# Row softmax without TensorE transposes for five batches, attention pieces placed behind the second product, and pair sums queued later

## The chip, the cores and the metric

The kernel runs on one core of a Trainium2 chip. The time is the device time of one execution in microseconds (us), the median of several runs. Engines: TensorE (PE; its weight loads are listed apart as PEld), VectorE (DVE), ScalarE (ACT), GpSimd (POOL) and SyncE (SP, which issues the DMAs here).

## The reference

```python
# attention between x [B=8, H=8, S=512, D=64] and state [B, H, Ns=32, D]
scores = scale * x @ state.T                    # [.., 512, 32], softmax over the 32 states
xread  = softmax(scores) @ state
scores2 = scale * state @ x.T                   # [.., 32, 512], softmax over the 512 tokens
sread  = softmax(scores2) @ x
y = concat([xread, sread], axis=2)              # then [B*544, 512] = [4352, 512]
h = relu(y @ w_in);  y = (h * h) @ w_out        # w_in 512x2048, w_out 2048x512
out = ((y @ w1) * (y @ w2)) @ w3 @ w_out2       # w1, w2 512x1024, w3 1024x1024, w_out2 1024x512
```

The weights come as 64-bit floats, x and state as 32-bit ones; the output is float32, 4352 x 512.

## The kernel before

All matrices are used as a high and a low part (`split`, L79: a ScalarE copy makes the high part, a VectorE subtraction the low part), and a product is three TensorE passes over these parts, 128x128 weights against 512 columns. The framework makes the order of each engine's instructions: it takes them by their place in the program text, but an instruction whose inputs are not ready in its model may be passed by a later one; on the chip each engine then runs its own list strictly in that order. `tc.issue_after(ins)` queues the instructions of a block that run on the engine of `ins` behind `ins`; instructions of the block on other engines are left alone.

**First stage.** The work goes in turns i = 0 to 143 over (c, f): c is a group of 512 token rows (one batch of `xread`, the ninth group is all of `sread`) and f one of 16 slices of 128 hidden columns. A turn does `h_tile(c, f)` (first product, six matmuls for c < 8, tile `ph`), then the jobs of `side[i]`, then `y_tile` of the turn two earlier (second product, twelve matmuls, tile `y`). From turn 32 on, c = i // 16. The side jobs are

- `conv` (L496): conversion of a 128x512 block of 64-bit weights by five VectorE and one or two ScalarE instructions, in every second turn from turn 24 on;
- `make_sw` (L349): product of the states with a block of `w_in`, sixteen matmuls of 64x32 weights into two PSUM banks, in turns f = 1, 5, 9, 13;
- the attention of batch b, spread by `att_slots(b)` (L336) over the sixteen turns of group c = b - 1, for b = 2 to 7. In slots 0 to 3 `xpose` (four TensorE transposes, `ps_x`), in 4 `scores`, in 5 and 7 `soft2`, in 7 and 11 `soft1a` (four transposes, `ps_n`, then two VectorE instructions), in 8 and 12 `soft1b`, in 10 and 13 `a_T` (four transposes, `ps_a`, then a `split`), in 6 and 10 `a2_T` (four transposes), in 8 and 11 `sread` (sixteen small matmuls), in 9 and 12 `sread_T` (one transpose). These steps stand in front of the other side jobs of their turn.

All of these pieces take their PSUM from one pair of banks, `bank_m` (L70, two buffers). A piece can start only when ScalarE or VectorE has emptied the bank that it gets; `make_sw` wants both.

The scores tile `S` holds, per half r, 4 heads x 32 states on the partitions and 512 tokens on the free axis. `soft1a` turns it so that tokens lie on the partitions and 32 states lie side by side on the free axis, and reduces over these 32.

**Last stage.** Groups go in pairs (2,3), (4,5), (6,7), (0,1), once for each half s of the hidden columns, in the second half in the opposite order. For a pair, `load_pair` (L667) reads eight blocks of y into two `wi1` buffers. Groups 0 and 1 lie in three parts each, so their pair also reads 16 further blocks through two `pt` buffers, which GpSimd adds (L676). `make_pair` (L680) makes seven sums and differences with eight VectorE subtractions and fourteen `split`s, 22 VectorE instructions in all. Four `quad`s (L714, m = 0 to 3, 42 matmuls each) multiply, and `out_tile` (L793, eight per pair, 12 matmuls each, two PSUM banks) makes the outputs. `load_pair` of the next pair stands behind quad m = 1, its `make_pair` behind the first of the eight output tiles; `make_w` stands there in place of `make_pair` between the halves.

Of the kernel before, what the change touches and what calls it, by code (L numbers as in the profile page):

```python
# [8 lines left out]
F32 = mybir.dt.float32  # L9
# [11 lines left out]
def kernel(  # L21
# [17 lines left out]
    nc = tc.nc  # L39
    B, H, S, D = x.shape  # L40
    NS = state.shape[2]
# [4 lines left out]
    P = 128  # L46
    G = 2
    HG = H // G
    J = S // P
    NF = DF // P  # L50
# [3 lines left out]
    NT9 = B * NS  # L54
    scale = 1.0 / float(D) ** 0.5
    HI, LO = 0, 1

    def f32(ap):
        return ap.bitcast(F32)
# [6 lines left out]
    ident = const.tile([P, P], F32, name="ident")  # L66
# [3 lines left out]
    def bank_m(name):  # L70
        return psum.tile([P, 512], F32, tag="m", bufs=2, name=name)
# [91 lines left out]
    def make_win0(half, kk):  # L163
        if win_t[0] is None:
            win_t[0] = wpool.tile([P, ND, 512], F32, tag="wi0", bufs=2, name="win0")
        convert64(("win0", half, kk), win_t[0][:, 2 * kk:2 * kk + 2, half * 256:(half + 1) * 256])
# [55 lines left out]
    def att_steps(b):  # L222
# [3 lines left out]
        v = {}  # L226
# [39 lines left out]
            v["a2", r] = e  # L266

        def soft1a(r):
            ps = bank_m("ps_n")
            for j in range(J):  # L270
                nc.tensor.transpose(ps[:, j * P:(j + 1) * P], v["S", r][:, j * P:(j + 1) * P], ident)
            pv = ps.rearrange("p (k n) -> p k n", n=NS)
            mx = att.tile([P, J * HG, 1], F32, tag="mx", bufs=2, name="mx")
            nc.vector.tensor_reduce(out=mx, in_=pv, axis=AX.X, op=ALU.max)
            e = att.tile([P, J * HG, NS], F32, tag="e1", bufs=1, name="e1")
            nc.vector.tensor_tensor(out=e, in0=pv, in1=mx.to_broadcast([P, J * HG, NS]), op=ALU.subtract)
            v["e1", r] = e

# [7 lines left out]
            nc.vector.tensor_tensor(out=e, in0=e, in1=sm.to_broadcast([P, J * HG, NS]), op=ALU.mult)  # L286

        def a_T(r):
            ps = bank_m("ps_a")
            e = v["e1", r].rearrange("p k n -> p (k n)")  # L290
            for j in range(J):
                nc.tensor.transpose(ps[:, j * P:(j + 1) * P], e[:, j * P:(j + 1) * P], ident)
            t = pa.tile([P, 2, 512], F32R, tag=f"aT{r}", bufs=2, name=f"aT{r}")
            split(t[:, HI], t[:, LO], ps)
            aT_t[b, r] = t
# [114 lines left out]
    def y_tile(c, f):  # L410
        n = 512 if c < B else NT9
        part, (f0, f1) = [(i, sg) for i, sg in enumerate(segs[c]) if sg[0] <= f < sg[1]][0]
        if f == f0:
            for d in range(ND):
                y_ps[c, d] = bank_y(d, f"y{d}")
        t = g_t.pop((c, f))
        for d in range(ND):
            for k, (wi, gi) in enumerate(PASSES):
                nc.tensor.matmul(  # L419
                    y_ps[c, d][:, :n], wo_t[f][:, wi, d * P:(d + 1) * P], t[:, gi, :n],  # L420
                    start=(f == f0 and k == 0), stop=(f == f1 - 1 and k == 2),
                )
            if f == f1 - 1:
                o = pa.tile([P, 512], F32, tag="yo", bufs=2, name="yo")
                if d % 2:
                    nc.vector.tensor_copy(o[:, :n], y_ps[c, d][:, :n])
                else:
                    nc.scalar.copy(o[:, :n], y_ps[c, d][:, :n])  # L428
                nc.sync.dma_start(y_scr[c][part][:, d, :], o[:, :n])
# [75 lines left out]
        return lambda: make_sw(b, fg)  # L505

    side = {i: [] for i in range(NF * B)}
    side[0] = [lambda: make_win0(1, 0), s2[0], lambda: make_win0(1, 1), xp1[0], xp1[1], a2t[0]]
    side[1] = [lambda: make_sw(0, 0, slice(256, 512)), lambda: make_wout(0), xp1[2], xp1[3], sr[0], s2[1], sc1]
    side[2] = [conv, s1a1[0], srt[0], a2t[1], s1b1[0], sr[1], at1[0]]  # L510
# [10 lines left out]
        side[i].append(conv)  # L521
    for b in range(2, B):
        for i, steps in enumerate(att_slots(b)):
            side[(b - 1) * NF + i] = steps + side[(b - 1) * NF + i]
        for fg in range(NFG):
            if (b, fg) != (B - 1, NFG - 1):
                side[b * NF + 4 * fg + 1].append(sw(*((b, fg + 1) if fg + 1 < NFG else (b + 1, 0))))
        for g in range(G):
            i = 9 + g if b == 2 else (b - 2) * NF + 12 + g
            side[i].append(lambda b=b, g=g: (load_x(b, g), make_x(b, g)))  # L530
# [27 lines left out]
    for i, (c, f) in enumerate(order):  # L558
        h_tile(c, f)

        with tc.issue_after(done[i - 3].ins) if i >= 8 else nullcontext():
            for job in side.get(i, ()):
                job()
        if c == B - 1 and f == 11:
            att_cm.__exit__(None, None, None)
            w34_cm = tc.tile_pool(name="w34p", bufs=1, reuse_waits="tile")
            w34p = w34_cm.__enter__()
            for j in range(N1 // 2):
                load_wo2(j)
        if c == B - 1 and f == NF - 1:  # L570
            split_x9(0)
            split_x9(1)
        if c == B:
            if f < N1:
                split_wo2(f)
            if f in (2, 4, 6, 8):
                load_w3(N1 // 2 + f // 2 - 1)
        pend.append((c, f))
        if len(pend) > 2:
            y_tile(*pend.pop(0))  # L580

    w3T = {}

# [124 lines left out]

    def to_c(c, m, q, n):
        t = bp.tile([P, 2, 512], F32R, tag="c", bufs=2 * QM, name="c")  # L710
        split(t[:, HI, :n], t[:, LO, :n], q)
        c_t[c, m] = t

    def quad(c0, c1, m):  # L714
        def product(ps, w, v, first=True, last=True):
            for kt in range(2):
                for k, (wi, vi) in enumerate(PASSES):
                    nc.tensor.matmul(  # L718
                        ps, W[w, kt][:, wi, m * P:(m + 1) * P], Y[v, kt][:, vi, :],
                        start=(first and kt == 0 and k == 0), stop=(last and kt == 1 and k == 2),  # L720
                        skip_group_check=True,
                    )

        def kept(i, ps):
            t = bp.tile([P, 512], F32, tag=f"s{i}", bufs=1 + (i == 0), name=f"s{i}")
            nc.scalar.copy(t, ps)  # L726
            return t

        def plus(t, ps):
            nc.vector.tensor_tensor(out=t, in0=ps, in1=t, op=ALU.add)  # L730

        A, D, E, C = bank_m("qa"), bank_y(m % 2, "qd"), bank_y(2, "qe"), bank_y(3, "qc")
        product(A, "A11", "B11", last=False)
        p1 = kept(0, A)
        product(D, "S1", "T1", last=False)
        p5 = kept(1, D)
        product(E, "A12", "B21")
        plus(p1, E)
        product(A, "S2", "T2", first=False, last=False)
        u2 = kept(2, A)  # L740
        product(D, "S4", "B22", first=False)
        plus(u2, D)
        product(C, "A22", "T4")
        product(A, "S3", "T3", first=False)
        u3 = kept(3, A)
        plus(p5, A)
        nc.vector.tensor_tensor(out=u2, in0=u2, in1=p5, op=ALU.mult)  # L747
        to_c(c1, m, u2, 512)
        plus(u3, C)
        nc.vector.tensor_tensor(out=p1, in0=p1, in1=u3, op=ALU.mult)  # L750
        to_c(c0, m, p1, 512)

    def load9():
        ts = []
# [89 lines left out]
    for s, todo in enumerate((pairs, pairs[::-1])):  # L844
        for i, (c0, c1) in enumerate(todo):
            for m in range(QM):
                quad(c0, c1, m)
                if m == 1 and i + 1 < len(todo):
                    raw = load_pair(*todo[i + 1])
                if m == 1 and i + 1 == len(todo) and s == 0:  # L850
                    raw = load_w(1)
            if i + 1 == len(todo) and s == 1:
                raw = load9()
            outs = [(c, t) for c in (c0, c1) for t in range(n_out(c))]
            if s == 1:
                for o in outs[:3]:
                    load_o(*o)
            for n, (c, t) in enumerate(outs):
                if s == 1 and n + 3 < len(outs):
                    load_o(*outs[n + 3])  # L860
                out_tile(c, t, s)
                if n == 0 and i + 1 < len(todo):
                    make_pair(raw)
                if n == 0 and i + 1 == len(todo) and s == 0:
                    make_w(raw)
                if n == 3 and i + 1 == len(todo) and s == 1:
                    make9(raw)
            if s == 0 and i + 1 == len(todo):
                for j in range(N1 // 4):
                    w34_t[N1 // 4 + j] = wpool.tile([P, 2, 2, DM], F32R, tag="wi0", bufs=2, name="w34b")  # L870
                    nc.sync.dma_start(f32(w34_t[N1 // 4 + j]), w34_s[j])
# [35 lines left out]
```

## Time and profile before

| | |
|---|---|
| median of 3 runs | 1330.67 us (1328.37 to 1331.24) |
| the profiled execution, its own time | 1329.5 us |
| its span, first to last instruction | 1327.7 us |
| mean granted TensorE clock | 0.985 |
| busy: PE / DVE / ACT / POOL | 1284.6 / 782.9 / 654.8 / 64.5 us |

The span lies 1.8 us under the profiled execution's own time; start and end of the program make the difference. Busy time is the time in which an engine had an instruction under way. Matmuls overlap and their ends are modelled, so PE may be listed as busy while the next matmul waits for its weights; the distance from one turn to the next shows such waits.

### The profile page before, as it was taken

How to read it: one execution, taken by the hardware profiler on the slowest of the kernel's cores; microseconds unless marked ns; L12 is line 12 of the kernel's file. 1: busy time of each engine (PE TensorE's matmuls, PEld its weight loads, DVE VectorE, ACT ScalarE, POOL GpSimd, SP SyncE). 2: the span in 40 equal slices, each digit the busy share in tenths (PEclk: the TensorE clock that was granted, in tenths of full speed). 3: DMA queues.
4: the chain of work that ended last, by engine and by line, in shares of the span. 5: the costliest groups of instructions: out<-in, count | busy, mean ns of one | idle time of the engine just before them, and what ended most of it. 6: DMA issues, size and time to landing. Idle time of an engine off the chain costs nothing.

```text
span 1327.7 us, 17120 instructions
## 1 busy us (share of the span) xinstructions
PE 1284.6 (97%) x6552; PEld 1012.7 (76%) x6552; DVE 782.9 (59%) x1388; ACT 654.8 (49%) x1190; POOL 64.5 (5%) x52
## 2 busy tenths in 40 slices
PE   3998999999999999999999999999799999999998
PEld 2666677777777777777789988888688888888877
DVE  6899875565656656543244764736273747567552
ACT  3765765656556565554565633525153533425121
POOL 0112300000000000000000000000500000000000
PEclk8898999999999999999999999999899999999999
DMA  6246534233242332300031342031502235050322
GB/s 205 65 129 223 172 103 135 96 103 104 81 149 72 105 117 80 103 9 1 33 127 64 108 162 79 18 110 60 179 32 96 78 129 163 28 191 9 119 70 89
DMA packets 65361, 132.70 MB, mean 100 GB/s; under 512 B 8704, under 2 KB 17408, under 8 KB 64768
## 3 DMA queue, kind: packets, MB, share of 16 engines
q1 hardware_dynamic: 65280, 131.62, 30.5%
q8 instruction: 51, 0.84, 0.2%
q14 instruction: 30, 0.25, 0.1%
HBM read 88.08 MB, written 43.52 MB: 99 GB/s over the span
## 4 chain that ended last, share of the span: by engine, by line
PE 86%; DVE 7%; DMA 3%; ACT 2%; issue 1%; POOL 1%; SPq 0%; POOLq 0%; DVEq 0%
PE y L419 25%; PE po L799 12%; PE qa L718 9%; PE qd L718 6%; PE ps_sw L354 3%; PE ps_w L603 3%; PE qc L718 3%; PE qe L718 3%; PE ab L773 2%; DMA yp<-yscr 1%; PE ps_r L309 1%; PE ps_x L232 1%; DVE ce L143 1%; DVE cm L140 1%; DVE ghl L84 1%
## 5 line engine op out<-in xcount | busy, mean ns | idle before, releaser
L419 PE MATMUL y<-ghl,wo 128*128 128x512 f32 (+1 forms) x1728 | 414.6, 386 | 5.4 <-ACT yo L428 5.0
L419 PEld LDWEIGHTS y<-ghl,wo 128*128 128x128 f32 x1728 | 304.8, 189 | 103.2 <-issue 24.7
L84 DVE TENSOR_TENSOR ghl<-r,ghl 128x512 fp32r<-128x512 f32 (+1 forms) x144 | 96.8, 672 | 150.7 <-ACT ghl L83 129.9
L718 PE MATMUL qa<-yq,wq 128*128 128x512 f32 x576 | 144.9, 390 | 0.0
L726 ACT COPY s<-qa 128x512 f32<-128x512 f32 x96 | 56.4, 588 | 146.7 <-PE qa L718 141.0
L718 PEld LDWEIGHTS qa<-yq,wq 128*128 128x128 f32 x576 | 108.5, 188 | 22.7
L718 PE MATMUL qd<-yq,wq 128*128 128x512 f32 x384 | 99.5, 393 | 8.3 <-ACT s L726 8.3
L799 PE MATMUL po<-w34b,c 128*128 128x512 f32 x408 | 95.9, 390 | 0.3 <-DVE o L808 0.3
L799 PE MATMUL po<-w,c 128*128 128x512 f32 x408 | 95.6, 390 | 0.0
L718 PEld LDWEIGHTS qd<-yq,wq 128*128 128x128 f32 x384 | 72.8, 190 | 23.9 <-ACT s L726 8.7
L371 ACT ACTIVATE r<-r 128x512 f32<-128x512 f32 (+1 forms) x144 | 88.2, 612 | 2.3
L799 PEld LDWEIGHTS po<-w34b,c 128*128 128x128 f32 x408 | 76.3, 188 | 17.1 <-DVE o L808 0.8
L799 PEld LDWEIGHTS po<-w,c 128*128 128x128 f32 x408 | 76.2, 188 | 16.4 <-ACT o L805 0.8
L83 ACT CAST ghl<-r 128x512 fp32r<-128x512 f32 (+1 forms) x144 | 86.2, 599 | 3.3
L136 ACT ACTIVATE ce<-ce,ebias 128x512 int32<-128x512 int32 x72 | 51.9, 724 | 31.2 <-DVE ce L135 31.0
L354 PE MATMUL ps_sw<-win,stT 64*32 64x512 f32 (+1 forms) x528 | 55.9, 595 | 1.6 <-DVE aT L84 0.8
L730 DVE TENSOR_TENSOR s<-qa,s 128x512 f32<-128x512 f32 x32 | 22.1, 690 | 59.3 <-ACT s L726 59.3
L143 DVE SCALAR_TENSOR_TENSOR ce<-raw,ce 128x512 int32<-128x512 int32 x72 | 50.9, 708 | 4.1 <-ACT ce L136 4.0
L140 DVE SCALAR_TENSOR_TENSOR cm<-raw,cm 128x512 f32<-128x512 uint32 x72 | 52.9, 735 | 0.6
L83 ACT CAST c<-s 128x512 fp32r<-128x512 f32 x64 | 38.9, 621 | 28.8 <-DVE s L747 28.2
L83 ACT CAST yq<-yraw 128x512 fp32r<-128x512 f32 x70 | 42.1, 624 | 16.0 <-PE qa L718 7.5
L718 PE MATMUL qc<-yq,wq 128*128 128x512 f32 x192 | 50.0, 396 | 0.0
(542 smaller groups left out, 1851.0 us busy)
## 6 DMA issues: line engine op xcount, KB each, us to landing
raw<-in_moe_w_dram SPq DMA_DIRECT2D x32, 512.0 KB, 4.1
yraw<-yscr SPq DMA_DIRECT2D x56, 256.0 KB, 4.7
raw<-in_moe_w_out_dram SPq DMA_DIRECT2D x24, 512.0 KB, 3.7
yscr<-yo SPq DMA_DIRECT2D x48, 256.0 KB, 3.0
oscr<-o SPq DMA_DIRECT2D x34, 256.0 KB, 3.0
opart<-oscr SPq DMA_DIRECT2D x34, 256.0 KB, 3.5
x<-in_x_dram SPq DMA_DIRECT2D x16, 512.0 KB, 4.0
out_dram<-o SPq DMA_DIRECT2D x32, 256.0 KB, 2.8
```

The lines of the kernel that those rows point to most:

```text
L83: nc.scalar.copy(hi, src)
L84: return nc.vector.tensor_tensor(out=lo, in0=src, in1=f32(hi), op=ALU.subtract)
L136: nc.scalar.activation(e, e, ACTF.Relu, bias=ebias, scale=8.0)
L140: nc.vector.scalar_tensor_tensor(out=f32(m), in0=lw, scalar=2.0**-32, in1=m, op0=ALU.mult, op1=ALU.add)
L143: nc.vector.scalar_tensor_tensor(out=e, in0=hw, scalar=-(2**31), in1=e, op0=ALU.bitwise_and, op1=ALU.bitwise_or)
L354: nc.tensor.matmul(pss[r][k * NS:(k + 1) * NS, cols], stT[rows, b, k, :], win_t[fg][rows, k, cols], start=True, stop=True, tile_position=( ...
L371: nc.scalar.activation(r[:, :n], r[:, :n], ACTF.Square)
L419: nc.tensor.matmul(y_ps[c, d][:, :n], wo_t[f][:, wi, d * P:(d + 1) * P], t[:, gi, :n], start=(f == f0 and k == 0), stop=(f == f1 - 1 and k ...
L603: nc.tensor.matmul(ps, t[:, wi, (j % 4) * P:(j % 4 + 1) * P], wo2_t[j][:, vi, :], start=(j == 0 and k == 0), stop=(j == N1 - 1 and k == 2),)
L718: nc.tensor.matmul(ps, W[w, kt][:, wi, m * P:(m + 1) * P], Y[v, kt][:, vi, :], start=(first and kt == 0 and k == 0), stop=(last and kt == ...
L726: nc.scalar.copy(t, ps)
L799: nc.tensor.matmul(ps, v[:, vi, t * P:(t + 1) * P], w[:, wi, :], start=(m == 0 and k == 0), stop=(m == QM - 1 and k == 2),)
```

## The change

Three things change. From batch 3 on, `soft1a` and `a_T` turn their tile by one VectorE instruction each that transposes every 32x32 block in place of four TensorE transposes into PSUM; 32 tokens take the place of 32 states within each block, so the 32 states of a token come to lie side by side, and the same instruction turns them back. The target of `a_T` is the `S` tile. Second, the attention steps of batches 2 to 7 move from the front of `side[i]` to a new list `late[i]`, which is issued behind `y_tile`, with the same `issue_after`. Third, in the last stage `load_pair` stands behind quad m = 0, not 1, and the VectorE instructions of `make_pair` and `make_w` are queued behind the last VectorE instruction of the pair's last quad.

```diff
+    BLK = 3
         def soft1a(r):
-            ps = bank_m("ps_n")
-            for j in range(J):
-                nc.tensor.transpose(ps[:, j * P:(j + 1) * P], v["S", r][:, j * P:(j + 1) * P], ident)
-            pv = ps.rearrange("p (k n) -> p k n", n=NS)
+            e = att.tile([P, J * HG, NS], F32, tag="e1", bufs=1, name="e1")
+            if b >= BLK:
+                nc.vector.transpose(out=e.rearrange("p k n -> p (k n)"), in_=v["S", r])
+                pv = e
+            else:
+                ps = bank_m("ps_n")
+                for j in range(J):
+                    nc.tensor.transpose(ps[:, j * P:(j + 1) * P], v["S", r][:, j * P:(j + 1) * P], ident)
+                pv = ps.rearrange("p (k n) -> p k n", n=NS)
             mx = att.tile([P, J * HG, 1], F32, tag="mx", bufs=2, name="mx")
             nc.vector.tensor_reduce(out=mx, in_=pv, axis=AX.X, op=ALU.max)
-            e = att.tile([P, J * HG, NS], F32, tag="e1", bufs=1, name="e1")
         def a_T(r):
-            ps = bank_m("ps_a")
             e = v["e1", r].rearrange("p k n -> p (k n)")
-            for j in range(J):
-                nc.tensor.transpose(ps[:, j * P:(j + 1) * P], e[:, j * P:(j + 1) * P], ident)
+            if b >= BLK:
+                ps = v["S", r]
+                nc.vector.transpose(out=ps, in_=e)
+            else:
+                ps = bank_m("ps_a")
+                for j in range(J):
+                    nc.tensor.transpose(ps[:, j * P:(j + 1) * P], e[:, j * P:(j + 1) * P], ident)
...
+    late = {}
     for b in range(2, B):
         for i, steps in enumerate(att_slots(b)):
-            side[(b - 1) * NF + i] = steps + side[(b - 1) * NF + i]
+            late[(b - 1) * NF + i] = steps
...
         if len(pend) > 2:
             y_tile(*pend.pop(0))
+        with tc.issue_after(done[i - 3].ins) if i >= 8 else nullcontext():
+            for job in late.get(i, ()):
+                job()
...
             for m in range(QM):
-                quad(c0, c1, m)
-                if m == 1 and i + 1 < len(todo):
+                last = quad(c0, c1, m)
+                if m == 0 and i + 1 < len(todo):
                     raw = load_pair(*todo[i + 1])
...
                 out_tile(c, t, s)
-                if n == 0 and i + 1 < len(todo):
-                    make_pair(raw)
-                if n == 0 and i + 1 == len(todo) and s == 0:
-                    make_w(raw)
+                with tc.issue_after(last.ins):
+                    if n == 0 and i + 1 < len(todo):
+                        make_pair(raw)
+                    if n == 0 and i + 1 == len(todo) and s == 0:
+                        make_w(raw)
```

`to_c` and `quad` now return the last `split`'s VectorE instruction, for `last`.

## Rows read from the trace of the kernel before

**Rows 1.** Page, busy time, share of the span and instructions of PE and DVE

```profile
PE 1284.6 (97%) x6552; PEld 1012.7 (76%) x6552; DVE 782.9 (59%) x1388; ACT 654.8 (49%) x1190; POOL 64.5 (5%) x52
```

**Rows 2.** Page, chain that ended last, shares of the span by engine

```profile
PE 86%; DVE 7%; DMA 3%; ACT 2%; issue 1%; POOL 1%; SPq 0%; POOLq 0%; DVEq 0%
```

**Rows 3.** Windows: length, then busy per engine, clock, DMA share, GB/s

```profile
297.75:379.63 81.88, 81.84 (x443) 60.77 (x442) 48.68 (x95) 47.88 (x84) 2.63 (x2) 1.00 0.33 103
912.30:983.60 71.30, 62.98 (x266) 51.39 (x265) 35.68 (x55) 25.69 (x47) 20.46 (x16) 0.93 0.37 111
1043.60:1103.50 59.90, 59.90 (x265) 49.47 (x265) 35.45 (x57) 27.46 (x50) 0.00 (x0) 1.00 0.33 114
957.50:963.00 5.50, 5.44 (x13) 4.28 (x14) 3.44 (x4) 1.21 (x3) 2.02 (x3) 0.50 0.25 76
```

**Rows 4.** Windows of single turns, first matmul of one `ph` to the next

```profile
302.32:308.88 6.56, 6.56 (x40) 4.11 (x38) 2.71 (x5) 4.40 (x8) 0.00 (x0) 1.00 0.24 90
323.67:329.00 5.33, 5.33 (x35) 3.48 (x34) 1.83 (x8) 4.24 (x8) 0.00 (x0) 1.00 0.09 32
...
333.58:338.15 4.57, 4.57 (x23) 3.77 (x22) 2.98 (x6) 2.97 (x5) 0.00 (x0) 1.00 0.32 112
338.15:343.48 5.33, 5.33 (x36) 4.15 (x34) 4.28 (x10) 2.58 (x4) 0.00 (x0) 1.00 0.32 98
343.48:349.61 6.13, 6.13 (x36) 3.78 (x35) 3.04 (x8) 3.60 (x6) 0.00 (x0) 1.00 0.13 45
349.61:354.58 4.97, 4.97 (x27) 4.21 (x26) 3.24 (x6) 2.60 (x5) 0.00 (x0) 1.00 0.49 148
354.58:360.29 5.71, 5.71 (x39) 4.55 (x38) 2.83 (x6) 2.46 (x5) 0.00 (x0) 1.00 0.03 11
360.29:364.53 4.24, 4.24 (x20) 3.44 (x19) 4.13 (x11) 2.49 (x5) 0.00 (x0) 1.00 0.14 22
364.53:371.47 6.94, 6.94 (x39) 4.03 (x38) 4.04 (x8) 3.80 (x7) 1.04 (x1) 1.00 0.52 176
371.47:375.55 4.08, 4.08 (x19) 3.38 (x18) 2.79 (x4) 1.85 (x3) 1.59 (x1) 1.00 0.33 87
140.66:147.54 6.88, 6.85 (x40) 4.03 (x38) 5.52 (x11) 5.40 (x11) 4.44 (x1) 1.00 0.80 264
```

**Rows 5.** Waits of PEld, 216 to 640 us: us in total, times, longest

```profile
PEld ps_sw L354 <- ACT xT L237: 3.3, 5, 0.7
PEld ps_sw L354 <- PE ps_rT L321: 2.7, 5, 0.5
```

**Rows 6.** Groups of VectorE instructions: busy us, mean ns, idle before

```profile
L137 DVE TENSOR_SCALAR cm<-raw 128x512 int32<-128x512 int32 x72 | 30.1, 417 | 0.0
L750 DVE TENSOR_TENSOR s<-s,s 128x512 f32<-128x512 f32 x32 | 23.0, 718 | 0.0
L426 DVE COPY yo<-y 128x512 f32<-128x512 f32 x24 | 16.4, 685 | 9.4 <-DMA yscr<-yo 9.3
```

**Rows 7.** Timeline, 912 to 963 us: start, length, instruction, idle before

```profile
916.18 1.28 DVE L84 TENSOR_TENSOR c<-s,c 128x512 fp32r<-128x512 f32 x2
...
921.71 0.32 SPq L672 DMA_DIRECT2D yraw<-yscr  x1
...
932.91 0.69 DVE L693 TENSOR_TENSOR ytmp<-yraw 128x512 f32<-128x512 f32 x1 [10.03 <-POOL yraw L676]
...
953.67 0.69 DVE L693 TENSOR_TENSOR ytmp<-yraw 128x512 f32<-128x512 f32 x1 [8.83 <-POOL yraw L676]
...
956.26 1.26 POOL L676 TENSOR_TENSOR yraw<-yraw,yp 128x512 f32<-128x512 f32 x1 [0.44 <-DMA yp<-yscr]
956.29 1.78 DVE L750 TENSOR_TENSOR s<-s,s 128x512 f32<-128x512 f32 x1
...
957.56 2.92 PE L718 MATMUL qd<-yq,wq 128*128 128x512 f32 x6 [8.32 <-ACT s L726]
...
962.27 1.27 POOL L676 TENSOR_TENSOR yraw<-yraw,yp 128x512 f32<-128x512 f32 x1 [1.89 <-DMA yp<-yscr]
```

More of the change, by code (lines that the diff above doesn't have):

```diff
@@ L710, in to_c @@
         t = bp.tile([P, 2, 512], F32R, tag="c", bufs=2 * QM, name="c")
-        split(t[:, HI, :n], t[:, LO, :n], q)
         c_t[c, m] = t
+        return split(t[:, HI, :n], t[:, LO, :n], q)
     def quad(c0, c1, m):
@@ L750, in quad @@
         nc.vector.tensor_tensor(out=p1, in0=p1, in1=u3, op=ALU.mult)
-        to_c(c0, m, p1, 512)
+        return to_c(c0, m, p1, 512)
     def load9():
```

## Prediction

> **What bounds the kernel now.** I read the page's busy times first: TensorE is at 97% and VectorE at 59% [rows 1]. Busy time alone does not say that TensorE sets the end, so the chain that ended last comes next: 86% of it is TensorE work, and no other engine has over 7% [rows 2]. Then I cut the span into stages. In the first stage the sixteen turns of one group take 81.88 us with TensorE busy throughout at the full clock, while VectorE and ScalarE are busy for 48.7 and 47.9 us of it [rows 3]. Here each microsecond that TensorE is spared ends the kernel a microsecond earlier, and VectorE has some 33 us in each group to give. In the last stage one pair takes 59.90 us without a gap, but the stretch of pair (6,7) takes 71.30 with TensorE busy for 62.98 [rows 3]. That is the one place there where something other than TensorE sets the pace.
>
> A turn cannot be judged by busy time, since a matmul that waits for its weights is listed as busy. I took the distance between turns instead [rows 4]. A turn with no side job that uses TensorE lasts 4.08 us. With `make_sw` alone it lasts 5.33, so the sixteen small matmuls cost 1.25. With four transposes alone (slot 7) it lasts 4.57, so four transposes cost 0.49. With the single transpose of `sread_T` (slot 12) it lasts 4.24, so that costs 0.16.
>
> Slots with two pieces show waits. Slot 1 has `xpose` and `make_sw`: 4.08 + 0.49 + 1.25 = 5.82, and it lasts 6.56, so 0.74 is waiting. Slot 9 has `sread_T` and `make_sw`: 5.49 against 6.13, waiting 0.64. Slot 13 has `a_T` and `make_sw`: 5.82 against 6.94, waiting 1.12. The waits of the weight loads name the cause: `ps_sw` waits for ScalarE to empty the `xpose` bank five times in five groups, up to 0.7 us, and for the `sread_T` bank five times, up to 0.5 us [rows 5]. It is the pair of PSUM banks, and not any engine's load.
>
> **The change part by part: transposes.** In groups c = 2 to 6 (batches 3 to 7) four sets of four transposes go: slot 7 saves 0.49; slot 10, where the set runs right behind that of `a2_T`, saves 4.97 - 4.57 = 0.40; slot 11, behind `sread`, saves 5.71 - 5.33 = 0.38; slot 13 saves 0.49. That is 1.76 us for each group, 8.8 us for five, from 80 transposes at 0.11 each. The Trainium skill, page "TensorE: Matmul & The Clock Gate", Part 4, puts a transpose at about 275 ns in one kernel's context. By that figure my estimate of this term would be 80 x 0.275 = 22 us in place of 8.8; the distances of the turns decide for 8.8.
>
> What VectorE gets is twenty block transposes of 128x512. The trace has none. The cheapest 128x512 pass on VectorE takes 0.42 us, the longest in the stretch shown 1.78 us (next to GpSimd) [rows 6, 7]. I take the plain copy's 0.685 us [rows 6], since a block transpose also reads one tile and writes one. That is 13.7 us in all (8.3 to 36), 2.7 in a group where VectorE idles for 33. It is free because the results are wanted late: `a_T` follows `soft1b` by two turns (over 9 us), and aT is needed when the next group begins. Without that cover each would cost its 0.69 directly, 13.7 us. The reductions and the `split` read SBUF in place of PSUM; I price that at nothing, since the copy from PSUM (685 ns) and the product from SBUF (718) lie within 0.04 us [rows 6].
>
> **Attention behind the second product.** `make_sw` now follows `h_tile` with no attention piece between them. The piece of the turn before ran ahead of `h_tile`, so its bank has the six matmuls, 1.36 us (six of the eighteen in 4.08), to be emptied, where it had none; a bank's copy takes about 0.6 us. The piece of the same turn has the twelve matmuls of the second product, 2.72 us, behind `make_sw`. So the waits should go: 0.74 + 0.64 + 1.12 = 2.50 us for a group, 12.5 for five. Batch 2, which keeps its transposes, has the same three meetings; there `xpose` and `make_sw` take 6.88 [rows 4], which is 1.06 too long, and with 0.64 and 1.12 as above 2.8 us in all. The new wait, `issue_after`, holds only VectorE instructions behind a low part made three turns earlier, which is long done. No DMA is in the moved steps. The conversions, now ahead of them on VectorE, occupy it for some 3 us every second turn; the attention results have a turn or more of slack against that. I take 0 for new waits between pieces; the upper bound is that of the waits in place now.
>
> **Pair sums later.** In the stretch of (6,7), VectorE stands at two subtractions of the next `make_pair` for 10.03 and 8.83 us, waiting for GpSimd's sums of the pair (0,1); behind them in its list are the quad's own sums. So the ScalarE copy that `qd` needs is late and TensorE stands for 8.32 us [rows 7]. After the stop it runs at the lower of its two levels, 1.2 GHz (granted 0.50), from 957.5 to 963 [rows 3]. Together that is 71.30 - 59.90 = 11.4 us. With the sums of (0,1) queued behind the pair's last quad, nothing in these quads waits for the load.
>
> What is late next? `make_pair` of (6,7) now starts behind the low parts of the last quad of (4,5), at about 916 where they end at 917.5 now [rows 7], with 22 instructions at 0.60 us from start to start (two take 1.28 [rows 7]), 13.3 us. It ends at 929.5, and only then are the buffers free for the load of (0,1), which starts at 921.7 now and ends with the last GpSimd sum at 963.5 [rows 7]. It then ends near 971, and standing at m = 0 in the text doesn't hasten it. The quads of (6,7) end at 972 without the stop, their VectorE tail at 976, `make_pair` at 989.5, and the eight output tiles cover it until 994. The cover is 4.5 us, and 8 us more for the operand that a quad wants last. The 24 loads share SP's queue with the last output stores of (4,5), as they do now; no other DMA stands behind them.
>
> The cost is at each of the seven changes of operands. The first product of the next pair can no longer fill TensorE while the last `c` tile is made; it filled six matmuls, 1.36 us. But VectorE then has three `make_pair` instructions fewer ahead of that tile, 1.8 us. Between 0 and 1.36 I take 0.2, so 1.4 us in all (0 to 9.5). In the second half eight output additions a pair stand behind `make_pair` on VectorE; 13.3 + 8 x 0.6 = 18.1 us fit the 21.8 us of output tiles, less the 4 us of tail, almost exactly.
>
> **Sum.** 8.8 + 12.5 + 2.8 + 11.4 - 1.4 = 34.1 us. The profiled execution's own time is 1329.5, and 1329.5 - 34.1 = 1295.4. The median of the runs shown lies 1.2 above it, so I say 1296.
>
> **The rivals.** *The bank waits stay.* The place in the text only sets a priority, and the copies that empty the banks may be queued behind a conversion. Then 15.3 us don't come: 1311. For it: such waits are what this order produces now. Against it: distances of 1.36 and 2.72 us against copies of 0.6.
>
> *The stop at (0,1) comes back in another form.* The load, 8 us later, may not be done, or GpSimd's sixteen sums may slow the quads' VectorE work beside them. The row shows it: a product of two SBUF tiles that takes 0.72 on average took 1.78 beside a sum that began 0.03 us before [rows 6, 7], 1.06 more. A quad has four such instructions, so at worst 4.2 us on top of some 5 of its 9.5 us; then VectorE would be just full. All 11.4 us given back make 1307. The Trainium skill, page "SBUF — State Buffer", section "Who interferes with whom", says that a VectorE instruction with two SBUF inputs and a GpSimd instruction that reads SBUF shut each other out for a whole instruction; the trace agrees, 1.78 against 0.72.
>
> *Both of these:* 1322.
>
> *Slower: the attention pieces stop the first product.* They now stand right ahead of the next `h_tile`. If a piece is not ready, everything behind it in TensorE's list waits, where before the second product's turn had the same fate. There are 11 such pieces in each of five groups and 15 in batch 2, 70 in all. At 34.1 / 70 = 0.49 us each the change is worth nothing; at the 0.74 that slot 1 waits now it takes 52 us: 1296 + 52 = 1348. For it: VectorE now has conversions ahead of attention work. Against it: every piece still has a full turn of over 4 us from its input's step.
>
> *The change doesn't do what it says:* the framework's order passes over the new places, and gains and new waits cancel: within 0.2% of before.
>
> **How the numbers follow.** Forecast 0.62, with a range of its own from 1290 (more of batch 2's waits go) to 1305 (operand changes at their upper bound); bank waits stay 0.13; the stop comes back 0.12; both 0.05; no net change 0.03; slower 0.05. The range 1288 to 1313 takes in the forecast and the first two rivals. Within 0.2%, 2.7 us, is about what a measurement of this kernel can't tell from no change. Faster 0.62 + 0.13 + 0.12 + 0.05 = 0.92, same 0.03, slower 0.05.
>
> **What would show it.** Turns with `make_sw` should last 5.33 to 5.82 us, slot 7 4.08, slot 13 5.33; rows of `ps_sw` waiting for `xT` or `ps_rT` should be gone; a group should take 77.6 us. A block transpose should be near 0.69 us. The stretch of (6,7) should take 60 us at a clock of 1.00, with the wait of L693 for GpSimd behind its last quad. I am wrong if turns without `make_sw` grow (TensorE waiting ahead of `ph`), if TensorE stops at the start of a pair's first quad, or if the output tiles stand behind the pair sums.

## The result and the profile after

The changed kernel takes 1310.17 us (median, 1309.04 to 1310.51) against 1330.49 us before: a ratio of 0.9848, 95% interval 0.9831 to 0.9865. It is faster by 20.3 us. That lies in the stated range, but outside the forecast's own 1290 to 1305, and 14 us above the time that I held likeliest.

The page's busy times and the chain's shares, as in [rows 1] and [rows 2]:

```profile
PE 1262.6 (97%) x6472; PEld 996.2 (76%) x6472; DVE 796.3 (61%) x1408; ACT 664.1 (51%) x1190; POOL 64.6 (5%) x52
...
PE 80%; DVE 10%; DMA 6%; ACT 3%; issue 1%; SPq 1%; DVEq 0%; ACTq 0%
```

80 transposes are gone from PE and 20 instructions are new on DVE. But PE's share of the chain fell from 86% to 80%, and DVE, DMA and ACT have more of it: the stage that was TensorE alone now waits for others in places.

Windows of the changed kernel: the turns of batch 2's attention (16 to 31), turn 21 of them, slots 1, 7, 9 and 13 of the group at 297.7, the whole group at 375.92, slot 2 of the group at 530.96, the stretch of pair (6,7), and a pair of the second half:

```profile
131.04:220.14 89.10, 82.00 (x443) 60.77 (x442) 66.85 (x122) 55.21 (x97) 14.29 (x8) 0.98 0.43 134
157.63:169.17 11.54, 7.61 (x42) 4.40 (x35) 9.16 (x18) 8.02 (x16) 3.19 (x2) 0.85 0.31 93
302.13:307.94 5.81, 5.81 (x42) 3.88 (x40) 2.19 (x4) 3.90 (x7) 0.00 (x0) 1.00 0.24 87
333.29:337.50 4.21, 4.21 (x21) 3.46 (x20) 0.98 (x4) 3.65 (x7) 0.00 (x0) 1.00 0.50 166
342.70:348.20 5.50, 5.50 (x37) 3.54 (x36) 3.22 (x7) 3.23 (x6) 0.00 (x0) 1.00 0.26 95
...
362.32:367.76 5.44, 5.44 (x36) 3.57 (x35) 2.32 (x6) 2.82 (x5) 1.04 (x1) 1.00 0.42 140
375.92:453.45 77.53, 77.53 (x427) 58.52 (x426) 50.50 (x99) 48.64 (x84) 2.38 (x2) 1.00 0.35 109
541.20:547.50 6.30, 4.90 (x25) 3.62 (x24) 3.74 (x8) 3.53 (x6) 0.00 (x0) 1.00 0.42 151
898.80:958.80 60.00, 60.00 (x266) 49.33 (x265) 36.29 (x54) 26.43 (x46) 21.24 (x16) 1.00 0.42 132
...
1079.30:1141.80 62.50, 60.87 (x266) 48.90 (x265) 38.80 (x62) 21.78 (x38) 0.00 (x0) 1.00 0.32 101
```

Against [rows 4], slot 1 went from 6.56 to 5.81, slot 7 from 4.57 to 4.21, slot 9 from 6.13 to 5.50 and slot 13 from 6.94 to 5.44. The group of [rows 3] went from 81.88 to 78.23, the five groups 2 to 6 together from 408.39 to 389.72, and the stretch of (6,7) from 71.30 [rows 3] to 60.00 at the full clock. These were the aims. Three things stand against them. Slot 2 takes 6.30 us in the group at 530.96 and 5.58 in that at 297.7, against 4.85 in the other three (4.55 to 4.88 in the kernel before). The first change of operands in the second half makes its pair take 62.50, where the pair ahead of it in [rows 3] and this pair too took 59.9 before. And turns 16 to 31 take 89.10, where the kernel before has this row:

```profile
131.54:216.19 84.65, 82.91 (x444) 60.76 (x443) 64.08 (x122) 53.68 (x97) 14.49 (x8) 1.00 0.43 141
```

Turn 21 alone went from 6.61 to 11.54 us. TensorE is listed with 7.61 us there, so it stood for some 4, and its mean granted clock in this turn is 0.85.

The waits of the weight loads from 216 to 640 us, as in [rows 5]:

```profile
PEld y L428 <- ACT yo L437: 3.3, 3, 1.8
...
PEld y L428 <- DVE yo L435: 2.2, 6, 0.6
PEld ps_sw L363 <- ACT S L252: 1.8, 5, 0.4
```

and two of the kernel before:

```profile
PEld y L419 <- DVE yo L426: 1.4, 3, 0.6
...
PEld y L419 <- ACT yo L428: 0.3, 1, 0.3
```

The state product no longer waits for `xT` or `ps_rT`. What is left is 0.4 us five times for the scores' banks (slot 5). Another wait has grown, from 1.7 to 5.5 us: the second product waits for the y banks of the group before to be copied out.

By span the kernel gained 20.0 us. It went like this, before minus after: up to turn 16 0.5; turns 16 to 31 -4.45; groups 2 to 6 18.66; group 7 0.0; the ninth group -1.1; output to output of the eight pair passes 6.2; the rest 0.2.

### The profile page after: what moved, and what is told of

It is laid out like the page before. It is cut to its first block, busy times and chain, and to the rows that moved or that the text cites. A ratio compares the mean times of both kernels' runs of the same rounds, so it can differ in the third digit from the quotient of the medians.

```text
span 1307.7 us, 16982 instructions
## 1 busy us (share of the span) xinstructions
PE 1262.6 (97%) x6472; PEld 996.2 (76%) x6472; DVE 796.3 (61%) x1408; ACT 664.1 (51%) x1190; POOL 64.6 (5%) x52
## 4 chain that ended last, share of the span: by engine, by line
PE 80%; DVE 10%; DMA 6%; ACT 3%; issue 1%; SPq 1%; DVEq 0%; ACTq 0%
PE y L428 24%; PE po L812 9%; PE qa L731 9%; PE qd L731 6%; PE ps_w L616 3%; PE qc L731 3%; PE qe L731 3%; PE ps_sw L363 2%; DMA yscr<-yo 2%; PE ab L786 2%; DVE yq L85 2%; DMA out_dram<-o 1%; PE ps_r L318 1%; DVE ce L144 1%; PE ps_x L233 1%
## 5 line engine op out<-in xcount | busy, mean ns | idle before, releaser
L428 PE MATMUL y<-ghl,wo 128*128 128x512 f32 (+1 forms) x1728 | 408.3, 383 | 11.4 <-ACT yo L437 8.4
L428 PEld LDWEIGHTS y<-ghl,wo 128*128 128x128 f32 x1728 | 309.8, 189 | 103.7 <-issue 14.3
L821 DVE TENSOR_TENSOR o<-po,opart 128x512 f32<-128x512 f32 x34 | 23.4, 691 | 45.7 <-PE po L812 22.5
L85 DVE TENSOR_TENSOR yq<-yraw,yq 128x512 fp32r<-128x512 f32 x70 | 47.0, 688 | 4.7 <-ACT yq L84 4.3
```

The costliest lines, as they stand in the source:

```text
L85: return nc.vector.tensor_tensor(out=lo, in0=src, in1=f32(hi), op=ALU.subtract)
L428: nc.tensor.matmul(y_ps[c, d][:, :n], wo_t[f][:, wi, d * P:(d + 1) * P], t[:, gi, :n], start=(f == f0 and k == 0), stop=(f == f1 - 1 and k ...
```

## Experiments

The first three do one part of the change alone.

**e1, transposes alone.** `soft1a` and `a_T` as in the change, all else as before.

```diff
+            if b >= BLK:
+                nc.vector.transpose(out=e.rearrange("p k n -> p (k n)"), in_=v["S", r])
...
```

> The kernel before with the block transposes on VectorE alone; nothing moved. By the terms of the prediction: 8.8 us for the 80 transposes, and 1.12 us in each of five groups because slot 13 then has no second piece that takes a bank: 14.4 us, a time of about 1316. Rival (the saving is only the transposes' own distance and a bank wait stays in slot 13): 8.8 us, about 1322.

1316.72 us, ratio 0.9897 (0.9882 to 0.9913): 14.5 us. The slot with a state product and no `a_T` on TensorE, slot 13:

```profile
279.61:284.95 5.34, 5.34 (x35) 3.48 (x34) 1.81 (x3) 2.82 (x5) 1.04 (x1) 1.00 0.48 167
```

5.34 against 6.94 [rows 4]: the 0.49 of four transposes and the 1.12 of the bank wait are both gone, by the transposes' going alone.

**e2, the later place alone.** `late` as in the change, transposes on TensorE.

```diff
-            side[(b - 1) * NF + i] = steps + side[(b - 1) * NF + i]
+            late[(b - 1) * NF + i] = steps
...
```

> The kernel before with the attention steps behind the second product alone. Theory A (batch 2 loses behind the conversions, groups 2 to 6 gain their 2.5 us less some 0.5 for the exchange of the y banks): +10 -4.5, so about 5 us faster, 1325. Rival B (the bank waits go only where the transposes are gone too): no gain in groups 2 to 6 and the loss in batch 2, 1330 to 1335.

1323.12 us, 0.9945 (0.9932 to 0.9957): 8.1 us. From the first matmul of turn 32 to that of turn 112 (groups 2 to 6) its profile has 396.5 us against 408.4 before, 11.9 less; turns 16 to 31 take 88.5, 3.9 more. Rival B falls. Its slots 2 take 4.85 us in all five groups, and none takes more. Slot 13 of one group and slot 1 of the next, with two pieces in each:

```profile
285.54:291.33 5.79, 5.79 (x40) 3.87 (x39) 4.74 (x10) 2.82 (x5) 1.14 (x2) 1.00 0.38 120
304.05:309.86 5.81, 5.81 (x42) 3.88 (x40) 2.19 (x4) 3.90 (x7) 0.00 (x0) 1.00 0.27 95
```

Both lie at the 5.82 of the pieces without a wait.

**e3, pair sums alone.**

```diff
+                with tc.issue_after(last.ins):
+                    if n == 0 and i + 1 < len(todo):
+                        make_pair(raw)
...
```

> The kernel before with the later pair sums and the earlier load alone. Theory A (the stop at (0,1) goes, 11.4 us, and each change of operands in the second half loses 1 to 3 us because output additions stand behind the pair sums): 6 to 7 us faster, about 1324. Rival (the second half's loss comes from the other parts): 10 to 11 us faster, about 1320.

1322.95 us, 0.9938 (0.9926 to 0.9951): 8.3 us, midway between the two, so the time doesn't decide. The trace does: the three changes of operands in the second half take 183.1 us together in its profile, where before they take 179.6. So the second half loses with this part alone.

**e4, batch 2 back in front.** The changed kernel, with

```diff
-            late[(b - 1) * NF + i] = steps
+            if b == 2:
+                side[(b - 1) * NF + i] = steps + side[(b - 1) * NF + i]
+            else:
+                late[(b - 1) * NF + i] = steps
```

> The changed kernel, but batch 2's attention steps stay in front of the other side jobs; batches 3 to 7 are behind the second product. Theory A: turns 16 to 31 take 84.7 us as before in place of 89.1, so 4.5 us faster than the changed kernel, about 1305.5. Rival (the stretch is slow because the conversions' loads are late whatever the order): 1310.

1305.21 us, 0.9806 (0.9793 to 0.982), 5 us under the changed kernel. Turns 16 to 31 take 84.2 us. Theory A holds.

**e5, later pair sums in the first half only.**

```diff
-                with tc.issue_after(last.ins):
+                with tc.issue_after(last.ins) if s == 0 else nullcontext():
```

> The changed kernel, but the pair sums are queued behind the last quad only in the first half (s = 0); in the second half they may run early, as before. Theory A (in the second half the output additions stand behind the 22 pair-sum instructions on VectorE, and the next quad waits for them): the three changes of operands there take 59.9 us a pair again in place of 62.7, 61.0 and 60.4; 4.4 us faster than the changed kernel, about 1306. Rival (the second half is slow because VectorE has too much there in any order): 1310.

1307.88 us, 0.9834 (0.982 to 0.9847). That is 2.3 us under the changed kernel and about half of what I expected; the intervals overlap. In the profile the three changes take 180.2 us against 183.9, so 3.7 come back there; but turn 16 begins 2.2 us later in it, in a stretch that the edit doesn't touch. The same pair as above:

```profile
1081.00:1140.80 59.80, 59.80 (x266) 49.50 (x265) 38.81 (x63) 21.19 (x38) 0.00 (x0) 1.00 0.33 106
```

VectorE has the same 38.8 us of work in this pair as in the changed kernel's, and TensorE loses nothing. It is the order, not the load. Over the profiles, the six kernels with the pair sums queued in the second half (the changed one, e3, e4, e7, e8, e9) take 182.3 to 185.4 us for the three; the eight without (before, e1, e2, e5, e6, e10, e11, e12) take 179.6 to 180.3.

**e6, both.** e4 and e5 together.

> Batch 2 in front (as e4) and the pair sums queued later in the first half only (as e5). Theory A: both losses are separate, 5.0 and 4.4 us, so about 1301. Rival (they share a cause, or one takes the place of the other): 1304 to 1306.

1303.08 us, 0.9798 (0.9784 to 0.9812): 2.1 us under e4, again less than its 4.4; the e4 and e6 intervals overlap. In the profiles the three changes take 182.3 us in e4 and 179.7 in e6, so only 2.7 were there to gain, and turns 16 to 31 take 84.15 in both. The two losses add; neither takes the place of the other.

**e7, batch 2 in front of the second product, but behind the conversions.**

```diff
-                side[(b - 1) * NF + i] = steps + side[(b - 1) * NF + i]
+                side[(b - 1) * NF + i] = side[(b - 1) * NF + i] + steps
```

> Batch 2's attention steps ahead of the second product, but behind the conversions of their turn; all else as changed. Theory A1 (it is the place behind the conversions on ScalarE's and VectorE's lists that makes the scores late): turns 16 to 31 take about 89 us and the time is that of the changed kernel, 1310. Theory A2 (it is the place behind the second product itself): 84 to 85 us, and 1305 as in e4.

1304.92 us, 0.9811 (0.9798 to 0.9825); turns 16 to 31 take 84.4 us. A2 holds. My first idea, that the rank behind the conversions was to blame by itself, falls: with the same rank but ahead of the second product nothing is lost.

**e8, every block transpose twice.**

```diff
...
-                nc.vector.transpose(out=ps, in_=e)
+                for _ in range(2):
+                    nc.vector.transpose(out=ps, in_=e)
```

> The changed kernel with every block transpose on VectorE made twice, one after the other, 20 more of 0.71 us. If VectorE's work there is covered: no change, 1310. Rival (the transposes lie on the path that ends last): up to 14 us slower, 1324.

1311.05 us, 0.9857 (0.9843 to 0.987), against 0.9848 (0.9831 to 0.9865): no difference in the time from 14 us more of VectorE work. The transposes are covered, or nearly: in its profile groups 2 to 6 take 390.83 us against 389.72, mostly as slot 9 goes from 5.50 to 5.74 or 5.75 in four of them.

**e9, batch 2's scores alone in front.** The changed kernel with one step of one batch back.

```diff
+            if (b, i) == (2, 4):
+                side[(b - 1) * NF + i] = steps + side[(b - 1) * NF + i]
+            else:
                 late[(b - 1) * NF + i] = steps
```

> The changed kernel, but of batch 2 the step of the scores alone (turn 20) stands in front of the other side jobs again. Theory (behind the second product the scores come so late that ScalarE's copies of them stand behind the next turn's conversion, and the state product of turn 21 waits for their banks): turn 21 falls from 11.5 us to about 6.5, so 4 to 5 us faster than the changed kernel, 1305 to 1306. Rival (the stretch is slow wherever the scores stand): 1310.

1304.8 us, 0.981 (0.9797 to 0.9824); turn 21 takes 5.33 us. Turns 16 to 31 take 84.25 us, so one step accounts for the whole loss of batch 2. The timeline of turns 20 and 21 in the changed kernel:

```profile
156.61 1.09 PE L246 MATMUL ps_s<-xT,stT 64*32 64x512 f32 x16
...
162.05 0.62 ACT L176 CAST wo<-cw 128x512 fp32r<-128x512 f32 x1 [2.58 <-DVE cw L147]
162.58 1.06 ACT L252 COPY S<-ps_s 128x512 f32<-128x512 f32 x2
...
163.21 2.26 PE L363 MATMUL ps_sw<-win,stT 64*32 64x512 f32 x16 [3.93 <-ACT S L252]
```

and in e9:

```profile
154.37 2.01 PE L246 MATMUL ps_s<-xT,stT 64*32 64x512 f32 x16
...
159.27 1.07 ACT L252 COPY S<-ps_s 128x512 f32<-128x512 f32 x2
160.22 0.63 ACT L176 CAST wo<-cw 128x512 fp32r<-128x512 f32 x1
...
160.66 1.09 PE L363 MATMUL ps_sw<-win,stT 64*32 64x512 f32 x16
```

In the changed kernel the scores come 2.2 us later, by the clock, and the framework sets ScalarE's copies of them behind a conversion's cast, which waits 2.58 us for VectorE. Scores that lay ready from 157.7 leave their banks at 163.6, and `ps_sw` stands for 3.93 us. In e9 the copies precede the cast.

**e10, block transposes for batch 2 too.** e6 with `BLK = 2`.

> As e6 (batch 2 in front, pair sums later in the first half only), with block transposes on VectorE for batch 2 too. Theory (TensorE sets the pace from turn 16 on too): 1.76 us for the transposes and about 1.1 for the bank wait of slot 13, so 3 us faster than e6, 1300. Rival (VectorE is full in turns 16 to 22, so its extra work returns the saving): 1303 or slower.

1299.47 us, 0.9766 (0.9753 to 0.978). The time is the one expected, the reason isn't. Turns 16 to 31 take 84.95 us, not less than the 84.14 of e6, although sixteen transposes fewer run there: turns 18, 25 and 26 (7.41, 7.23 and 6.42 us, in e6 6.57, 6.16 and 5.19) give the saving back. What its profile gains comes from slots 2 of two groups and the start of the ninth, where e6 takes 5.98, 5.76 and 5.36 us and e10 4.84, 4.84 and 3.85, with the same order there. The timeline of such a slot in the changed kernel and in e10 shows the difference:

```profile
540.47 5.44 SPq L438 DMA_DIRECT2D yscr<-yo  x3
...
544.98 0.58 ACT L437 COPY yo<-y 128x512 f32<-128x512 f32 x1 [1.91 <-DMA yscr<-yo]
...
545.62 1.70 PE L428 MATMUL y<-ghl,wo 128*128 128x512 f32 x6 [1.40 <-ACT yo L437]
```

```profile
536.74 3.43 SPq L438 DMA_DIRECT2D yscr<-yo  x3
...
539.23 0.59 ACT L437 COPY yo<-y 128x512 f32<-128x512 f32 x1
```

The third copy of a y bank needs one of two `yo` buffers back from its store. It starts 4.5 us after that store's issue in the one and 2.5 in the other. The changed kernel's DMA view from 540 to 546 us shows what ran beside the slow store:

```profile
q8 instruction: 1, 0.02, 2.0%
...
yscr<-yo SPq DMA_DIRECT2D x3, 256.0 KB, 4.0
```

The first row is a load of the program's own instructions, a transfer of 1.9 us from 541.48 on. In e10 none runs beside that store, which lands 2.1 us after its issue.

It is so in every trace. In nine kernels (the changed one, e2, e4 to e10) groups 2 to 6 have 45 slots 2 of this order. In 14 of them an instruction load runs beside the first store; it lands after 3.7 to 4.4 us and the slot takes 5.58 to 6.30. In the other 31 the store lands after 2.0 to 2.1 us and the slot takes 4.83 to 4.86. The ninth group's turn takes 3.85 us in the five kernels of all fourteen that have no such load there, and 4.83 to 5.54 in the nine that have one, e1 among them, where nothing was moved; e2, where the steps were, has none and takes 3.85.

So this part of e10's gain depends on where the instruction loads fall; no run shifts one alone. The two profiled executions of e6 and e10 lie only 1.0 us apart (1301.13 and 1300.14): the three places give 3.6 us, turns 16 to 31 take 0.8 back and the last two changes of the first half 1.7.

**e11, slot 1's state product one turn later.** e6, with

```diff
-                side[b * NF + 4 * fg + 1].append(sw(...))
+                side[b * NF + 4 * fg + (2 if fg == 0 else 1)].append(sw(...))
```

> As e6, with the state product of slot 1 moved to slot 2, the turn in which the second product of a group begins. Theory (that turn lasts 0.3 to 1.7 us too long because the y banks are not emptied in time; ScalarE's state copies stand ahead of the bank copies, and there are two buffers for the stores): turn 2 loses its wait and TensorE has 1.25 us more work ahead of the new y, so 2 to 4 us faster than e6, 1299 to 1301. Rival (the product meets the conversions of the even turns and waits itself): 1303 to 1306.

1298.11 us, 0.9761 (0.9747 to 0.9774), 5 us under e6. Slot 2, now with the state product in it:

```profile
302.17:307.96 5.79, 5.79 (x42) 3.88 (x40) 5.24 (x10) 4.42 (x8) 0.00 (x0) 1.00 0.65 186
```

It lies at 5.79 to 5.81 us in all five groups, the sum of its pieces, and every group takes 77.2 us. In the profiles groups 2 to 6 gain 3.3 us over e6; 2.0 of them lie in the two slots 2 where e6's stores met an instruction load, which e11's don't.

**e12, both.**

> e6 with both: block transposes from batch 2 on and the state product of slot 1 in slot 2. If both gains hold and add: 1297. If only one holds: 1300.

1297.49 us, 0.9756 (0.9743 to 0.9769): the fastest, but not to be told from e11. The gains don't add; both lie in slots 2, at the same wait for the y banks. It is 12 to 13 us under the changed kernel and 1.5 us above the time that I had forecast for that one.

## Why the prediction was right and where it failed

**That the time lies in the range is luck in part.** The range reaches to 1313 because it took in two rivals, at 1307 and 1311, and neither happened. The terms for the transposes, the bank waits of groups 2 to 6 and the stop held where they were tested alone (e1, e2, e3), and 14 us were lost to new waits, which the prediction had priced at 0, and at the changes of operands, priced at 1.4. Nothing in the prediction's working kept this loss inside the range.

**Transposes: right.** The terms for slots 7, 10, 11 and 13 with slot 13's wait give 14.4 us, and e1 measured 14.5. A block transpose takes this in the changed kernel:

```profile
L297 DVE STREAM_TRANSPOSE S<-e 128x512 f32<-128x512 f32 x10 | 7.1, 709 | 0.1
L272 DVE STREAM_TRANSPOSE e<-S 128x512 f32<-128x512 f32 x10 | 7.1, 705 | 0.0
```

0.71 us against the 0.685 that I took, and covered but for about 1 us at twice the work (e8).

The rule that I set against this term, the 275 ns for a transpose in the Trainium skill, page "TensorE: Matmul & The Clock Gate", Part 4, would by my estimate have made 22 us; e1's 14.5 contains the 5.6 of the bank waits, so the trace's 0.11 us each stands.

**Bank waits: right in groups 2 to 6.** 12.5 us forecast, 11.9 in e2, with the 0.3 that slots 2 lost in three groups in it. Rival "the bank waits stay" didn't happen.

**The stop at (0,1): right.** 11.4 us forecast, 71.30 to 60.00 measured. The load's delay was right too. The first load and the last GpSimd sum of the changed kernel:

```profile
916.08 0.32 SPq L685 DMA_DIRECT2D yraw<-yscr  x1
```

```profile
954.23 1.32 POOL L689 TENSOR_TENSOR yraw<-yraw,yp 128x512 f32<-128x512 f32 x1 [0.39 <-DMA yp<-yscr]
```

This part of the kernel now runs 13.5 us earlier, so on the clock of before the load starts at 929.6 and ends at 969; I had 929.5 and 971. Of 25 two-input VectorE instructions beside the sums, 21 take 0.71 us at most and four take 1.00 to 1.80, this one the longest:

```profile
952.60 1.80 DVE L85 TENSOR_TENSOR c<-s,c 128x512 fp32r<-128x512 f32 x1
```

So the slowdown of [rows 7] is there, but rare, and TensorE has no gap. That rival fell.

**What failed, first: "I take 0 for new waits between pieces", in batch 2.** The term was +2.8 us and measured -4.45, 7.3 us off. I reckoned with conversions every second turn, which holds from turn 24 on. In turns 16 to 22 there is one in each turn and two in some. In the kernel before VectorE is busy there for 33.8 of 38.3 us, so it has little to give, and ScalarE's list is what counts. The mechanism is a cousin of the slower rival, at one place: a piece not emptied in time, with the next product behind it. e9 shows that the scores' place alone does it. The +2.8 doesn't come even so: e9 gains 0.4. Turn 25's 0.63 and turn 29's 1.14 went as forecast, but turn 18's 1.06 stayed (6.88 before, 7.09 in the changed kernel) and turn 26 went from 5.28 to 7.11; in both the second product now waits for the y banks, 1.3 and 1.8 us.

**Second: the changes of operands, priced at 1.4 us, measured at 5.2** (6.2 us gained over the pairs in place of 11.4). In the first half the first two cost 0.1 each, under the 0.2 taken, and the third 0.6; the change to the second half's weights cost 0.1. In the second half they cost 4.3 together. I had the right count, 18.1 us of VectorE work for about 17.8 of cover, and let it pass with "almost exactly", while the order inside it decided. The changed kernel, at the first of these changes:

```profile
1085.08 0.69 DVE L821 TENSOR_TENSOR o<-po,opart 128x512 f32<-128x512 f32 x1
...
1097.12 0.69 DVE L821 TENSOR_TENSOR o<-po,opart 128x512 f32<-128x512 f32 x1
...
1105.80 0.69 DVE L821 TENSOR_TENSOR o<-po,opart 128x512 f32<-128x512 f32 x1 [3.85 <-DMA out_dram<-o]
...
1110.47 0.59 ACT L739 COPY s<-qd 128x512 f32<-128x512 f32 x1 [13.21 <-DVE o L821]
...
1115.37 1.65 PE L731 MATMUL qa<-yq,wq 128*128 128x512 f32 x6 [1.49 <-ACT s L739]
```

The second output addition stands 12 us behind the first, since the pair sums have the higher rank. The additions are then paced by two output buffers and their stores. They also read from the `s1` and `s2` buffers (`load_o`), so a `quad` that TensorE had begun early can't keep its first results there: ScalarE waits 13.21 us for an addition, and TensorE for ScalarE. My list of signs had "the output tiles stand behind the pair sums"; I gave it no price. e5 undoes it.

**Third, not in the sum: the y banks.** In slot 2 a new group's second product needs the old group's banks. The change took out the wait of 0.74 us that stood ahead of it, so these banks have that much less time, and ScalarE has the state product's copies first. Slots 2 took 3.05 us more over five groups, part of which the other slots gave back (groups 2 to 6: 18.66 in place of 21.3), and the ninth group 1.1. This has two parts. The 4.85 us in place of 4.55 comes with the new order in every kernel that has it, and e11 shows that it is a wait: with other TensorE work ahead it is gone. The 5.58 and 6.30 us and the ninth group's 1.1 come where an instruction load runs beside the stores (e10). None of e11's slots 2 met such a load, so whether its order would cover that longer wait too is not shown.

The shortfalls in batch 2, at the pairs (5.2 in place of 1.4), in groups 2 to 6 and in the ninth, 7.3 + 3.8 + 2.7 + 1.1 = 14.9, less 0.7 gained at the start and end, make up the 14.1 us between 34.1 and 20.0.

**Open.** That an instruction load makes the store slow is read from where the two meet; no run moved such a load by itself. The last two changes of the first half, 0.7 us here, were not taken apart; they cost 0.2 us in e6 and 2.4 in e11, which differ only in the first stage. A third `yo` buffer was not tried.

## What to carry to other kernels

When TensorE sets the pace, price a removed piece by the distance between turns with and without it; here that gave the terms to within 0.6 us, also for the bank waits. When steps are moved in an engine's order, check each stretch by itself for what is ahead of them on the engines that empty their banks: the same move gained 2.4 us a group where VectorE was busy for 60% of the time and lost 4 us in the turns where it was busy for 76%. And where two kinds of work just fit the cover, ask which of them comes first, and who shares a buffer with the other.

## What the runs showed that I had not expected

With the state product's waits gone, slot 2 began to wait in every group (4.85 us at least, where three of the five took 4.55 before): a wait had given cover to the next one. And a gain of the expected size can have another cause: e10 was 3.6 us under e6 as forecast, with none of it in the turns that its edit touches. What its profile gained over that of e6 lay where e6's stores met an instruction load and its own didn't, which neither edit was meant to change.
